# An attention and two-layer MoE kernel: scaled words in PSUM, joined maxima, numerator by head, and an order from a table

## The chip, the cores and the metric

The kernel runs on one core of a Trainium2 chip. The metric is the device time of one execution in microseconds (us), taken as the median of several runs.

## The reference

Random-feature attention gives the input of a gated MLP, whose output goes through eight experts with one expert per token. Cut to what matters (B 4, H 8, S 576, D 64, 128 features; 2304 tokens, model width 512, hidden widths 1536 and 1024; all float32):

```python
def phi(x):
    proj = np.einsum('bhsd,df->bhsf', x, w_phi)
    proj = proj - np.max(np.abs(proj), axis=-1, keepdims=True)
    return np.concatenate([np.exp(proj), np.exp(-proj)], axis=-1)
q_p, k_p = phi(q), phi(k)
kv = np.einsum('bhsf,bhsd->bhfd', k_p, v); z = np.sum(k_p, axis=2)
attn = np.einsum('bhsf,bhfd->bhsd', q_p, kv) / (np.einsum('bhsf,bhf->bhs', q_p, z)[..., None] + 1e-06)
x = attn.transpose(0, 2, 1, 3).reshape(B * S, H * D)
g = x @ moe_w_gate
x = (g / (1 + np.exp(-g)) * (x @ moe_w_val)) @ moe_w_out
# then, per token: e = argmax(x @ moe2_w_gate); gate * sigmoid(...) * relu(x @ w1[e]) @ w2[e]
```

## The kernel before

**Attention** goes by 16 units of two heads (u = 0 to 15; four units are one batch). A unit has: three *qk groups* (`qk_mm`, L286: projections of three 128-token tiles of q and of k into two PSUM banks); for each group the maximum of the absolute value and the subtraction on DVE (`amax` L294, `k_sub` L299, `q_sub` L309), where in the first part the q side of odd units takes its subtraction on ACT instead (`q_bias`, L314, three Identity instructions with a bias); two exponentials of the k side on ACT (`k_exp`); the *kv product* (`kv_mm`, L338 and L347) and its copy (`kv_copy`); three *transpose groups* of q (`tq_mm`, L365), each with two exponentials on ACT (`tq_exp`); the *numerator* (`num_mm`, L387 and L390), whose two banks hold six and four slices, since the tile shared by both heads is done for both; `normalise` (L403, L404, L407: an addition, a reciprocal and the products on DVE); the *output transposes* (`tx_mm`, L422), of which ACT keeps the rounded high part (`x_hi`) and DVE the rest (`x_lo`, L440).

**The gated MLP** goes by six blocks of 384 tokens (n) and twelve slices of the hidden width (f). Each slice has a *G product*, a *V product* (`gv_mm`, L540 to L542, 12 matmuls each) and an *o product* (`o_mm`, L578 to L580, 9 matmuls), each with a high and a low word of weights and of inputs. Between them lie `g_tanh` (ACT), `g_mul` (L552) and `v_mul` (L555) on DVE, `g_hi` (L558, ACT) and `g_lo` (L561), which makes the low word: on POOL in block 0, on DVE later. G and V have one bank each (3 and 4), the o products banks 0 to 2. Before a product, `split_hi` (L522, ACT) and `split_lo` (L526, POOL) cut the weights in two words; four buffers of each are in turn.

**Conversion.** The weights arrive as 64-bit words with three staging buffers (`conv_load`, SP). For each of 36 pieces ACT scales the high word into a buffer in SBUF (`conv_scale`, L491); the low word is rounded by POOL for the first eight pieces, by ACT for the others (`conv_round`, L498, L500); DVE joins sign and mantissa in two instructions (`conv_bits`, L504 and L505); POOL adds the two parts (`conv_add`, L509).

**The first part** (`first_part`) holds units 0 to 7, the qk groups of unit 8, all conversions and block 0 up to its last V product and the o product of slice 10. The G product of block 0 needs the outputs of units 0 to 3. Its order on PE, DVE, ACT and POOL is written by a planner (`Plan`): each step has a duration, a due time and what it reads and writes; at each turn the step that can start first is taken, among those that could start about then the one due first. Where PE would be idle for long before a certain time, a filler puts matmuls without use (L459). SP's loads are issued by the steps: `qk_mm` of the third group loads the next unit but one, `kv_mm` the values, `conv_load` the weights; SP takes them in one queue.

**After it** come blocks 1 to 5, into which units 8 to 15 are put step by step (`run_to`), then the routing and the expert slots.

Of the kernel before, what the change touches and what calls it, by code (L numbers as in the profile page):

```python
# [65 lines left out]


class Plan:
# [32 lines left out]
    def run(self, filler):
        ops = self.ops
        left = [len(o["deps"]) for o in ops]
        after = [[] for _ in ops]
        for i, o in enumerate(ops):
            for d in o["deps"]:
                after[d].append(i)
        end = [0.0] * len(ops)
        free = {}
        bank_free = [0.0] * 8  # L110
        ready = {i for i, n in enumerate(left) if n == 0}
        while ready:
            best = None
            for i in ready:
                o = ops[i]
                t = max([free.get(o["eng"], 0.0)] + [end[d] + self.LAT * (ops[d]["eng"] != o["eng"]) for d in o["deps"]])
                if o["banks"]:
                    b = sorted((bank_free[b], b) for b in o["pool"])[:o["banks"]]
                    if b[-1][0] == float("inf"):
                        continue  # L120
                    t = max(t, b[-1][0] + self.LAT)
                    o["take"] = [x[1] for x in b]
                cand = (t, o["due"], i)
                o["at"] = t
                if best is None or cand < best:
                    best = cand
            assert best is not None, "no op can be taken"
            same = [(ops[i]["due"], i) for i in ready if ops[i]["eng"] == ops[best[2]]["eng"]
                    and ops[i].get("at", 1e9) <= best[0] + 0.05 and (not ops[i]["banks"] or all(
# [997 lines left out]
```

## Time and profile before

| | us |
|---|---|
| median of 3 runs | 946.39 (945.83 to 946.68) |
| profiled execution | 945.33 |
| its span, first to last instruction | 943.6 |
| PE, DVE, ACT, POOL busy | 908.5, 640.8, 578.2, 404.6 |

The profile is that of one execution. A busy time says how long an engine had an instruction in work; matmuls are pipelined, and their modelled ends overlap, so the work of a group of matmuls is better read from its start to the start of the next group. Times in the trace are counted from the span's start.

### The profile page before, as it was taken

The numbers are of one execution on the slowest core, as the hardware profiler recorded it, in microseconds if no ns is written. First come the engines' busy times: TensorE is split into PE (matmuls) and PEld (weight loads), VectorE is DVE, ScalarE is ACT, GpSimd is POOL, SyncE is SP. The second block draws the span as 40 slices with busy tenths as digits, with TensorE's granted clock in tenths as the row PEclk, the third lists the DMA queues.
The fourth block names the chain that finished last, engine by engine and source line by source line (L and its number), as shares of the span: only waits on it lengthen the run. The fifth ranks groups of instructions, "written<-read, shape, count | busy, mean of one in ns | idle before, by whom it ended". The sixth has DMA issues, their size and how long they took to land.

```text
span 943.6 us, 18408 instructions
## 1 busy us (share of the span) xinstructions
PE 908.5 (96%) x7159; PEld 790.2 (84%) x7159; DVE 640.8 (68%) x1094; ACT 578.2 (61%) x1020; POOL 404.6 (43%) x324
## 2 busy tenths in 40 slices
PE   8998997999999999999999999989999999999995
PEld 5887886889999899988889999979877888887874
DVE  4899899645454744575564533565599988888984
ACT  4776876644545345454445344444588998888883
POOL 1459788735554344433435566566201111112210
PEclk9999999999999999999999999999999999999998
DMA  7555655120011101110000000054001137156240
GB/s 217 157 168 154 176 155 155 42 73 1 1 27 49 39 5 39 41 60 16 1 2 34 1 1 1 35 213 178 34 24 46 38 130 294 53 206 227 65 177 9
DMA packets 20939, 78.88 MB, mean 84 GB/s; under 512 B 5358, under 2 KB 5614, under 8 KB 19056
## 3 DMA queue, kind: packets, MB, share of 16 engines
q1 hardware_dynamic: 17280, 67.60, 22.2%
q0 software_dynamic: 3200, 9.48, 3.1%
q8 instruction: 58, 0.95, 0.4%
q10 hardware_dynamic: 368, 0.59, 0.2%
q14 instruction: 33, 0.27, 0.1%
HBM read 123.23 MB, written 10.00 MB: 141 GB/s over the span
## 4 chain that ended last, share of the span: by engine, by line
PE 76%; DVE 15%; issue 4%; DMA 3%; ACT 2%; POOL 0%; POOLq 0%; DVEq 0%; ACTq 0%
PE banks L915 10%; PE banks L540 10%; PE banks L542 9%; PE banks L541 9%; PE banks L578 5%; PE banks L579 5%; PE banks L580 5%; PE banks L286 3%; DVE arena L505 3%; PE banks L937 3%; PE banks L938 3%; PE banks L939 3%; DVE arena L504 2%; PE banks L347 2%; PE banks L390 2%
## 5 line engine op out<-in xcount | busy, mean ns | idle before, releaser
L526 POOL TENSOR_TENSOR arena_r<-arena,arena_r 128x512 fp32r<-128x512 f32 x216 | 285.8, 1325 | 247.2 <-ACT arena_r L522 234.4
L522 ACT ACTIVATE arena_r<-arena 128x512 fp32r<-128x512 f32 x216 | 135.9, 630 | 191.2 <-PE banks L541 109.7
L540 PE MATMUL banks<-arena_r 128*128 128x384 f32 x576 | 201.6, 350 | 1.7 <-DVE arena L552 1.0
L881 DVE TENSOR_TENSOR arena_r<-arena,arena_r 128x1024 fp32r<-128x1024 f32 x160 | 189.6, 1234 | 18.0 <-ACT arena_r L880 16.8
L542 PE MATMUL banks<-arena_r 128*128 128x384 f32 x576 | 193.9, 337 | 4.5 <-POOL arena_r L526 4.5
L541 PE MATMUL banks<-arena_r 128*128 128x384 f32 x576 | 193.4, 336 | 0.0
L880 ACT ACTIVATE arena_r<-arena 128x1024 fp32r<-128x1024 f32 x160 | 161.9, 1066 | 15.3 <-PE banks L915 10.9
L915 PE MATMUL banks<-arena_r 128*128 128x512 f32 x480 | 116.8, 396 | 0.0
L943 POOL DMA_INDIRECT out_dram<-arena x20 | 20.7, 1037 | 219.5 <-ACT arena L942 219.5
L540 PEld LDWEIGHTS banks<-arena_r 128*128 128x128 f32 x576 | 108.3, 188 | 7.8 <-issue 1.4
L542 PEld LDWEIGHTS banks<-arena_r 128*128 128x128 f32 x576 | 108.1, 188 | 5.8 <-POOL arena_r L526 5.8
L552 DVE SCALAR_TENSOR_TENSOR arena<-arena,banks 128x384 f32<-128x384 f32 x72 | 39.7, 552 | 107.6 <-ACT arena L549 107.5
L541 PEld LDWEIGHTS banks<-arena_r 128*128 128x128 f32 x576 | 108.5, 188 | 1.6
L915 PEld LDWEIGHTS banks<-arena_r 128*128 128x128 f32 x480 | 88.1, 188 | 20.2 <-ACT arena_r L907 2.1
L578 PE MATMUL banks<-arena_r 128*128 128x512 f32 x216 | 90.0, 417 | 0.0
L579 PE MATMUL banks<-arena_r 128*128 128x512 f32 x216 | 86.6, 401 | 0.0
L580 PE MATMUL banks<-arena_r 128*128 128x512 f32 x216 | 86.5, 402 | 0.0
L561 DVE TENSOR_TENSOR arena_r<-arena,arena_r 128x384 fp32r<-128x384 f32 x60 | 60.9, 1015 | 27.7 <-ACT arena_r L558 27.5
L294 DVE TENSOR_REDUCE arena<-banks 128x3 f32<-128x384 f32 x96 | 52.7, 554 | 23.6 <-PE banks L286 21.5
L555 DVE TENSOR_TENSOR arena<-arena,banks 128x384 f32<-128x384 f32 x72 | 39.8, 552 | 39.6 <-PE banks L542 38.8
L937 PE MATMUL banks<-arena_r 128*128 128x512 f32 x160 | 62.7, 392 | 1.0 <-ACT arena_r L880 0.7
L939 PE MATMUL banks<-arena_r 128*128 128x512 f32 x160 | 62.4, 390 | 0.0
(126 smaller groups left out, 1434.6 us busy)
## 6 DMA issues: line engine op xcount, KB each, us to landing
arena<-mw SPq DMA_DIRECT2D x40, 2048.0 KB
ov_conv<-w1cat SPq DMA_DIRECT2D x24, 512.0 KB
arena<-w1cat SPq DMA_DIRECT2D x12, 512.0 KB
arena<-v SPq DMA_DIRECT2D x16, 325.0 KB
x2d<-arena SPq DMA_DIRECT2D x18, 256.0 KB
arena<-qT SPq DMA_DIRECT2D x15, 288.0 KB
arena<-kT SPq DMA_DIRECT2D x15, 288.0 KB
ov_gather<-x2d,arena POOLq DMA_INDIRECT x20, 3.8
```

The lines of the kernel that those rows point to most:

```text
L522: ACT.activation(WH[i % 4], WR[f][w], AF.Copy)
L526: POOL.tensor_tensor(out=WL[i % 4], in0=WR[f][w], in1=WH[i % 4].bitcast(F32), op=ALU.subtract)
L540: PE.matmul(ps, wh[:, c], xh, start=(k == 0), stop=False)
L541: PE.matmul(ps, wh[:, c], xl, start=False, stop=False)
L542: PE.matmul(ps, wl[:, c], xh, start=False, stop=(k == 3))
L578: PE.matmul(ps, GH[f % 2][:, ts_], woh, start=(f == 0), stop=False)
L579: PE.matmul(ps, GH[f % 2][:, ts_], wol, start=False, stop=False)
L580: PE.matmul(ps, GL[f % 2][:, ts_], woh, start=False, stop=(f == NFT - 1))
L880: ACT.activation(h, src, AF.Copy)
L881: DVE.tensor_tensor(out=l, in0=src, in1=h.bitcast(F32), op=ALU.subtract)
L915: PE.matmul(PS[:, HB[h], :], lhs, w[:, h * 512:(h + 1) * 512], start=a, stop=b)
L937: PE.matmul(ps, HTH[:, k, :], wh[:, cs], start=(k == 0), stop=False)
```

## The change

- `conv_scale` writes the scaled word into a bank of PSUM, and `conv_bits` reads it there. The buffers CU go; CP becomes four buffers. The rounding runs on ACT or, where the table says so, on POOL.
- q and k of a qk group lie in two adjacent banks. One reduction takes the maxima of both, one subtraction serves both (`qk_sub`), into one tile KQ. `q_bias` goes. The sign of q's exponentials is exchanged accordingly.
- `num_mm` and `normalise` go by head, five slices each, with one bank each.
- `v_mul` writes its product back into the V bank; `g_hi` and `g_lo` read it there; `g_lo` is on DVE in all blocks.
- `Plan.run` no longer chooses: it takes the steps in the order of a list of 626 numbers, in which 1000 more than a step's number means its other engine (POOL for the rounding, DVE for the copy of kv). Durations and the delay between engines still serve to choose banks and fillers. A bank is chosen by when it comes free; outside the first part, by which was used longest ago.

With the table, DVE's order ahead of the first product of block 0 (now the V product) has 15 `qk_sub`, 9 `conv_bits`, 8 `normalise`, 8 `x_lo` and one copy of kv; PE's has 17 qk groups, 15 transpose groups, 5 kv products, the numerators and the output transposes of units 0 to 3. The second V product comes after three G products. The cut diff:

```diff
-NRP = 8
...
+PLAN_TABLE = [242, 247, 2, 1, 252, 0, 3, 4, 7, 5, 10, 13, 8, 6, 17, 33, 18, 11, 36, 9, 19, 20, 34, 39, 12, 21, 42, 22,
...
+    615, 606, 616, 617, 621, 613, 622, 614, 623, 618, 624, 619, 625, 620, 239, 240, 241]
...
+    def run(self, table, filler):
+        ops, lat = self.ops, self.LAT
+        end, on, free, bank_free = {}, {}, {}, [0] * 8
+        assert sorted(x % 1000 for x in table) == list(range(len(ops)))
+        for x in table:
+            i = x % 1000
             o = ops[i]
-            ready.discard(i)
-            filler(o["eng"], free.get(o["eng"], 0.0), o["at"])
+            eng, dur, fn = o["alt"] if x >= 1000 else (o["eng"], o["dur"], o["fn"])
+            assert all(d in end for d in o["deps"]), (i, o["deps"])
+            t = max([free.get(eng, 0)] + [end[d] + lat * (on[d] != eng) for d in o["deps"]])
             if o["banks"]:
-                o["holder"]["ps"] = [b for b in o["take"]]
-                for b in o["take"]:
-                    bank_free[b] = float("inf")
-                o["fn"](*o["take"])
-            elif o["holder"] is not None:
-                o["fn"](*o["holder"]["ps"])
-            else:
-                o["fn"]()
-            end[i] = o["at"] + o["dur"]
-            free[o["eng"]] = end[i]
+                if o["banks"] == 1:
+                    b = min(self.SINGLES, key=lambda b: max(t, bank_free[b] + lat))
+                else:
+                    b = min(self.PAIRS, key=lambda b: max(t, bank_free[b] + lat, bank_free[b + 1] + lat))
+                take = list(range(b, b + o["banks"]))
+                t = max([t] + [bank_free[b] + lat for b in take])
+            for b in o["claim"]:
...
+            fn(*(h["ps"][:1] if h is not None else ()))
+            on[i] = eng
+            end[i] = free[eng] = t + dur
...
-    CU = [buf(512) for _ in range(2)]
     CA = buf(512)
-    CP = [OV1[:, 2048:2560], buf(512)]
+    CP = [OV1[:, 2048:2560]] + [buf(512) for _ in range(3)]
...
+    def pair_no():
+        state["n"] += 1
+        b = min((b for b in state["banks"] if b + 1 in state["banks"]),
+                key=lambda x: (max(used[x], used[x + 1]), min(used[x], used[x + 1])))
+        used[b] = used[b + 1] = state["n"]
+        return b
...
-    def amax(b, m=MX):
-        ps3 = PS[:, b, :BT].rearrange("p (j f) -> p j f", f=P)
-        DVE.tensor_reduce(out=m, in_=ps3, axis=AX.X, op=ALU.max, apply_absolute_value=True)
-        return ps3, m.rearrange("p (j o) -> p j o", o=1).to_broadcast([P, 3, P])
-
-    def k_sub(u, c, b):
-        ps3, mb = amax(b)
-        DVE.tensor_tensor(out=KP[two(u)][:, 3 * c:3 * c + 3, 0:P], in0=ps3, in1=mb, op=ALU.subtract)
+    def qk_sub(u, c, b):
+
+        ps = PS[:, b:b + 2, :BT].rearrange("p w (j f) -> p w j f", f=P)
+        DVE.tensor_reduce(out=MX, in_=ps, axis=AX.X, op=ALU.max, apply_absolute_value=True)
+        t = KQ[two(u)][:, 3 * c:3 * c + 3, :].rearrange("p j (w f) -> p w j f", f=P)[:, 0:3:2]
+        m = MX.rearrange("p w (j o) -> p w j o", o=1).to_broadcast([P, 2, 3, P])
+        DVE.tensor_tensor(out=t, in0=ps, in1=m, op=ALU.subtract)
...
-    def q_sub(u, c, b):
-        ps3, mb = amax(b)
-        DVE.tensor_tensor(out=TQ[two(u)][:, 3 * c:3 * c + 3, :], in0=mb, in1=ps3, op=ALU.subtract)
-
-    def q_bias(u, c, b):
-        ps3 = PS[:, b, :BT].rearrange("p (j f) -> p j f", f=P)
-        for j in range(3):
-            ACT.activation(TQ[two(u)][:, 3 * c + j, :], ps3[:, j, :], AF.Identity, bias=MQ[c][:, j:j + 1], scale=-1.0)
...
+    def num_mm(u, h, b):
+
         kv = KV[u % 2]
-        for part, n in ((0, 6), (1, 4)):
-            ps = PS[:, banks[part], :n * 65].rearrange("p (s d) -> p s d", s=n)
-            for i in range(5 - part):
-                t = 5 * part + i
-                for a in range(2):
-                    for g in HALVES:
-                        q = qp(u)[:, a, t * P + g.start:t * P + g.stop]
-                        if t == 4:
-                            PE.matmul(ps[g, 4:6, :].rearrange("p s d -> p (s d)"), q, kv[:, a, :], start=(a == 0),
-                                      stop=(a == 1), skip_group_check=True)
-                        else:
-                            PE.matmul(ps[g, i, :], q, kv[:, a, part * 65:part * 65 + 65], start=(a == 0),
-                                      stop=(a == 1), skip_group_check=True)
+        ps = PS[:, b, :325].rearrange("p (s d) -> p s d", d=65)
+        for i in range(5):
+            for a in range(2):
+                for g in HALVES:
+                    t0 = h * S + i * P + (0 if i == 4 and h == 1 else g.start)
+                    PE.matmul(ps[g, i, :], qp(u)[:, a, t0:t0 + 64], kv[:, a, h * 65:h * 65 + 65], start=(a == 0),
+                              stop=(a == 1), skip_group_check=True)
...
+    def normalise(h, b):
+        ps = PS[:, b, :325].rearrange("p (s d) -> p s d", d=65)
+        rd = rot("rd", RD)[:, :5].rearrange("p (s o) -> p s o", o=1)
         DVE.tensor_scalar(out=rd, in0=ps[:, :, 64:65], scalar1=1e-6, scalar2=None, op0=ALU.add)
         DVE.reciprocal(out=rd, in_=rd)
-
-        def norm(dst, rows, s0, s1):
-            DVE.tensor_tensor(out=dst, in0=ps[rows, s0:s1, 0:64],
-                              in1=rd[rows, s0:s1].to_broadcast([rows.stop - rows.start, s1 - s0, 64]), op=ALU.mult)
-
-        lo, hi = slice(0, 64), slice(64, 128)
-        if part == 0:
-            norm(XT[:, 0:4, 0:64], slice(0, P), 0, 4)
-            norm(XT[lo, 4:5, 0:64], lo, 4, 5)
-            norm(XT[lo, 0:1, 64:128], hi, 5, 6)
-        else:
-            norm(XT[hi, 0:4, 64:128], lo, 0, 4)
-            norm(XT[lo, 1:5, 64:128], hi, 0, 4)
+        DVE.tensor_tensor(out=XT[:, :, h * 64:h * 64 + 64], in0=ps[:, :, 0:64], in1=rd.to_broadcast([P, 5, 64]), op=ALU.mult)
...
-    def conv_scale(i):
-        ACT.activation(CU[i % 2], ST[i % 3].rearrange("p (n two) -> p n two", two=2)[:, :, 1], AF.Copy,
+    def conv_scale(i, b):
+        ACT.activation(PS[:, b, :], ST[i % 3].rearrange("p (n two) -> p n two", two=2)[:, :, 1], AF.Copy,
                        scale=2.0 ** -112)
...
-        r = CP[i % 2].bitcast(I32)
-        if i < NRP:
+        r = CP[i % 4].bitcast(I32)
+        if eng is POOL:
...
-    def conv_bits(i):
-        ui, ai, wi = CU[i % 2].bitcast(I32), CA.bitcast(I32), WR[i // 3][i % 3].bitcast(I32)
+    def conv_bits(i, b):
+        ui, ai, wi = PS[:, b, :].bitcast(I32), CA.bitcast(I32), WR[i // 3][i % 3].bitcast(I32)
         DVE.tensor_scalar(out=ai, in0=ui, scalar1=-2 ** 31, scalar2=None, op0=ALU.bitwise_and)
         DVE.scalar_tensor_tensor(out=wi, in0=ui, scalar=3, in1=ai, op0=ALU.logical_shift_left, op1=ALU.bitwise_or)
...
-        DVE.tensor_tensor(out=GP, in0=GP, in1=PS[:, VB, :BT], op=ALU.mult)
+        DVE.tensor_tensor(out=PS[:, VB, :BT], in0=GP, in1=PS[:, VB, :BT], op=ALU.mult)
 
     def g_hi(f):
-        ACT.activation(GH[f % 2], GP, AF.Copy)
-
-    def g_lo(f, eng=DVE):
-        eng.tensor_tensor(out=GL[f % 2], in0=GP, in1=GH[f % 2].bitcast(F32), op=ALU.subtract)
+        ACT.activation(GH[f % 2], PS[:, VB, :BT], AF.Copy)
+
+    def g_lo(f):
+        DVE.tensor_tensor(out=GL[f % 2], in0=PS[:, VB, :BT], in1=GH[f % 2].bitcast(F32), op=ALU.subtract)
...
+                op("DVE", 190, lambda b, c=c: qk_sub(u, c, b), [("qk", u, c)] + tail, [("kp", z, c), ("tq", z, c)], holder=h, due=d0 + c)
+                op("ACT", 106, lambda c=c: k_exp(u, c), tail, [("kp", z, c)], due=d0 + c)
...
-            op("ACT", 0.69, due, lambda i=i: conv_scale(i), [("st", i % 3)], [("cu", i % 2)])
-            op("POOL" if i < NRP else "ACT", 1.65 if i < NRP else 0.69, due + 0.5, lambda i=i: conv_round(i), [("st", i % 3)], [("cp", i % 2)])
-            op("DVE", 1.75, due + 1, lambda i=i: conv_bits(i), [("cu", i % 2)], [("wr", i)])
-            op("POOL", 1.37, due + 3, lambda i=i: conv_add(i), [("cp", i % 2)], [("wr", i)])
+                op(("dma", i), 1400 + 300 * i, lambda: None, [], [("st", i % 3)])
+            h = op("ACT", 69, lambda b, i=i: conv_scale(i, b), [("st", i % 3)], [("cu", i)], 1, due=due)
+            op("ACT", 69, lambda i=i: conv_round(i, ACT), [("st", i % 3)], [("cp", i % 4)], due=due,
+               alt=("POOL", 162, lambda i=i: conv_round(i, POOL)))
+            op("DVE", 125, lambda b, i=i: conv_bits(i, b), [("cu", i)], [("wr", i)] + [("wrt",)] * (i >= 24), holder=h, due=due)
+            op("POOL", 137, lambda i=i: conv_add(i), [("cp", i % 4)], [("wr", i)], due=due)
...
-                op("DVE", 0.55, at + 1, v_mul, [("V",)], [("gp",)])
-                op("ACT", 0.53, at + 1.5, lambda f=f: g_hi(f), [("gp",)], [("gh", f % 2)])
-                op("POOL", 1.05, at + 2, lambda f=f: g_lo(f, POOL), [("gp",), ("gh", f % 2)], [("gl", f % 2)])
+                op("PE", 217, lambda f=f: gv_mm(0, f, 1), wts + xs, [("V",)], due=at)
+                op("DVE", 56, v_mul, [("gp",)], [("V",)], due=at)
+                op("ACT", 53, lambda f=f: g_hi(f), [("V",)], [("gh", f % 2)], due=at)
+                op("DVE", 60, lambda f=f: g_lo(f), [("V",), ("gh", f % 2)], [("gl", f % 2)], due=at)
...
-            ends = pl.run(filler)
+            pl.run(PLAN_TABLE, filler)
```

## Rows read from the trace of the kernel before

**Rows 1.** The page, part 1: busy us and share of the span by engine.

```profile
PE 908.5 (96%) x7159; PEld 790.2 (84%) x7159; DVE 640.8 (68%) x1094; ACT 578.2 (61%) x1020; POOL 404.6 (43%) x324
```

**Rows 2.** Windows: length, then busy us per engine, granted clock, DMA share, GB/s.

```profile
9.00:64.30 55.30, 50.64 (x914) 42.44 (x914) 47.82 (x108) 41.48 (x99) 22.22 (x16) 0.97 0.61 179
64.30:169.00 104.70, 92.84 (x816) 80.36 (x815) 98.19 (x142) 76.75 (x162) 88.52 (x66) 0.97 0.53 155
169.00:200.00 31.00, 31.00 (x308) 27.40 (x308) 18.69 (x38) 18.05 (x40) 18.47 (x15) 1.00 0.19 50
200.00:600.00 400.00, 399.32 (x3404) 362.72 (x3403) 204.13 (x441) 188.94 (x383) 189.84 (x149) 1.00 0.08 24
```

**Rows 3.** Timeline of PE: start us, length us, engine, line, count.

```profile
9.04 1.16 PE L286 MATMUL banks<-arena 64*128 64x128 f32 x16
...
64.31 0.42 PE L540 MATMUL banks<-arena_r 128*128 128x384 f32 x1
...
173.33 0.94 PE L286 MATMUL banks<-arena 64*128 64x128 f32 x12
174.20 0.55 PE L365 MATMUL banks<-arena 128*128 128x128 f32 x3
174.50 0.48 PE L578 MATMUL banks<-arena_r 128*128 128x512 f32 x1
...
180.65 0.45 PE L540 MATMUL banks<-arena_r 128*128 128x384 f32 x1
...
185.04 1.15 PE L390 MATMUL banks<-arena 128*64 128x65 f32 x32
...
187.50 0.50 PE L578 MATMUL banks<-arena_r 128*128 128x512 f32 x1
...
189.68 0.71 PE L422 MATMUL banks<-arena 128*128 128x128 f32 x5
```

**Rows 4.** Groups by line on PE, to 64.3 us, the last to 190.5 us.

```profile
L286 PE MATMUL banks<-arena 64*128 64x128 f32 x180 | 14.4, 296 | 1.7 <-ACT arena L314 1.3 <-ACT arena L370 0.3
L347 PE MATMUL banks<-arena 128*64 128x65 f32 x320 | 10.2, 221 | 0.0
L390 PE MATMUL banks<-arena 128*64 128x65 f32 x256 | 9.0, 223 | 0.0
...
L286 PE MATMUL banks<-arena 64*128 64x128 f32 x301 | 25.3, 295 | 4.2 <-DVE arena_r L440 2.5 <-ACT arena L314 1.3 <-ACT arena L370 0.3
```

**Rows 5.** Groups by line and shape, 0 to 200 us: busy us, mean ns.

```profile
L505 DVE SCALAR_TENSOR_TENSOR arena<-arena 128x512 int32<-128x512 int32 x36 | 44.5, 1236 | 1.2
L504 DVE TENSOR_SCALAR arena<-arena 128x512 int32<-128x512 int32 x36 | 33.0, 918 | 3.3 <-ACT arena L491 2.4
L294 DVE TENSOR_REDUCE arena<-banks 128x3 f32<-128x384 f32 x54 | 29.4, 552 | 16.0 <-PE banks L286 14.8
...
L314 ACT ACTIVATE arena<-banks,arena 128x128 f32<-128x128 f32 x36 | 10.4, 360 | 0.5 <-DVE arena L294 0.5
...
L440 DVE TENSOR_TENSOR arena_r<-banks,arena_r 128x192 fp32r<-128x192 f32 x16 | 5.2, 349 | 1.9 <-ACT arena_r L436 1.8
...
L440 DVE TENSOR_TENSOR arena_r<-banks,arena_r 128x384 fp32r<-128x384 f32 x4 | 2.2, 554 | 1.3 <-ACT arena_r L436 1.3
...
L404 DVE RECIPROCAL arena<-arena 128x6 f32<-128x6 f32 x8 | 1.5, 192 | 0.3
```

**Rows 6.** Timeline of DVE, one pair of conv_bits.

```profile
62.71 0.43 DVE L504 TENSOR_SCALAR arena<-arena 128x512 int32<-128x512 int32 x1
63.17 1.66 DVE L505 SCALAR_TENSOR_TENSOR arena<-arena 128x512 int32<-128x512 int32 x1
```

**Rows 7.** Timeline of POOL at the same time.

```profile
63.01 1.27 POOL L526 TENSOR_TENSOR arena_r<-arena,arena_r 128x512 fp32r<-128x512 f32 x1 [1.05 <-ACT arena_r L522]
```

**Rows 8.** Groups by line on DVE, 200 to 600 us.

```profile
L715 DVE COPY arena<-banks 128x512 f32<-128x512 f32 x13 | 9.0, 691 | 10.1 <-PE banks L714 10.1
```

**Rows 9.** Timelines of DVE and PE in a later block: g_lo, the next V product.

```profile
307.63 1.14 DVE L561 TENSOR_TENSOR arena_r<-arena,arena_r 128x384 fp32r<-128x384 f32 x1 [0.59 <-ACT arena_r L558]
...
315.08 0.44 PE L540 MATMUL banks<-arena_r 128*128 128x384 f32 x1
```

More of the change, by code (lines that the diff above doesn't have):

```diff
@@ L97, in op @@
             holder["users"] += 1
-        self.ops.append(dict(eng=eng, dur=dur, due=due, fn=fn, deps=deps, banks=banks, pool=pool, holder=holder))
+        self.ops.append(dict(eng=eng, dur=dur, fn=fn, deps=deps, banks=banks, holder=holder, claim=claim, alt=alt, due=due))
         return holder
[L101 to L129, printed above, removed]
-                        bank_free[b] < float("inf") for b in ops[i].get("take", ())))]
-            i = min(same)[1]
@@ new lines, in run @@
+                take = list(range(b, b + o["banks"]))
+                t = max([t] + [bank_free[b] + lat for b in take])
+            for b in o["claim"]:
+                t = max(t, bank_free[b] + lat)
+            assert t < self.NEVER, "no bank"
+            filler(eng, free.get(eng, 0), t)
+            for b in o["claim"]:
+                bank_free[b] = self.NEVER
+            h = o["holder"]
+            if o["banks"]:
+                h["ps"] = take
+                for b in take:
+                    bank_free[b] = self.NEVER
@@ L152, in run @@
                         bank_free[b] = h["end"]
-            for j in after[i]:
-                left[j] -= 1
-                if left[j] == 0:
-                    ready.add(j)
-        assert not any(left)
-        self.end = end
-        return free
+            if PLAN_LOG is not None:
+                PLAN_LOG.append((i, eng, t, dur))
 @with_exitstack
@@ L335, in kv_mm @@
                 for g in HALVES:
-                    lhs = KP[two(u)][:, t, a * P + g.start:a * P + g.stop]
+                    lhs = KQ[two(u)][:, t, a * P + g.start:a * P + g.stop]
                     if i == 0:
@@ L613, in unit @@
[L613 to L616 removed]
+            h = op("PE", 242, lambda b: kv_mm(u, b), [("kp", z, c) for c in range(3)] + [("v", u)] + tail,
+                   [("kvm", u)], 1, due=d0 + 8)
@@ L617, in unit @@
+            for p_ in range(2):
+                h = op("PE", 122, lambda b, p_=p_: num_mm(u, p_, b),
+                       [("qp", z, c) for c in ((0, 1), (1, 2))[p_]] + [("kv", u % 2)] + tail, [("num", u, p_)], 1,
+                       due=d0 + 14)
+                op("DVE", 85, lambda b, p_=p_: normalise(p_, b), [("num", u, p_)], [("xt", p_), ("xt2", p_)],
+                   holder=h, due=d0 + 14)
             for part in range(2):
```

159 lines of the change are left out of this document (72 added, 87 removed), and 25 rows, old and new, of the table PLAN_TABLE.

## The prediction

> **What bounds the kernel now.** I read the page first: PE is busy in 96% of the span [rows 1], so only time in which PE works on nothing needed can be won. The windows say where that is [rows 2]. From 200 to 600 us PE is busy 399.32 of 400 us: nothing to win. From 9 to 64.3 us and from 64.3 to 169 us it isn't, and there DVE is busy 47.82 of 55.3 and 98.19 of 104.7 us (94%), the highest share of any engine behind PE. From 169 us DVE falls to 18.69 of 31 and PE is at 31.00 of 31. So the first part is held by DVE until about 169 us, and then by PE.
>
> PE's busy time counts filler matmuls and overlapped ends, so I count from start to start in a dense stretch [rows 3]: a qk group (12 records) 174.20 - 173.33 = 0.87 us, a transpose group 174.50 - 174.20 = 0.30, two G or V products 185.04 - 180.65 = 4.39, so 2.19 each, a numerator 187.50 - 185.04 = 2.46 (a kv product has as many matmuls of the same widths and is taken at 2.46 too), an o product 189.68 - 187.50 = 2.18, a unit's output transposes 0.71.
>
> The first G product starts at 64.31, the last o product of the first part ends at 189.68 [rows 3]. By 64.3 us 180 qk records (15 groups) and the kv records of five units (320) and numerator records of four (256) are done, by 190.5 us 301 (25 groups) [rows 4]. Between the two marks PE had 24 x 2.19 + 11 x 2.18 + 10 x 0.87 + 3 x 2.46 (kv) + 4 x 2.46 (num) + 9 x 0.30 + 3 x 0.71 = 107.3 us of work in 125.4 us: it lost 18.1 us. Two qk groups and one unit's transposes of the first part are still owed then (2.4 us), so its work ends, in effect, at 192.1.
>
> **The change part by part.** DVE prices come from one view [rows 5]. An instruction with one PSUM operand takes 349 ns at 128x192 and 554 at 128x384, so 205 ns for 192 elements more: by that line 128x320 is 0.49 us, 128x512 0.69, 128x768 0.96.
>
> *Scaled words in PSUM.* The two instructions of conv_bits take 918 and 1236 ns on average, 77.5 us in all, and they vary: 0.43 and then 1.66 us in one pair [rows 6]. During the long one POOL ran a subtraction on SBUF words, 63.01 to 64.28 [rows 7]. With the scaled word in PSUM neither instruction reads two SBUF words any more. I take 0.691 (a 128x512 copy out of PSUM [rows 8]) for the first and 0.69 for the second: 1.38 against 2.15, 36 x 0.77 = 27.9 us less on DVE. Bounds: 1.12 (0.43 + 0.69) and 2.15; the copy is the nearest row. Here a rule speaks against the change: the Trainium skill, VectorE: DVE Perf Modes, section "Why PSUM operands drop a tier", says that an fp32 operand in PSUM holds such an instruction to the single rate. By that rule it is 0.69 and not the 0.43 of the SBUF form, and the copy's 0.691 agrees; with 0.43 the first G product would come 9 x 0.26 = 2.3 us sooner than below. ACT's write into PSUM has no row; ACT is busy for 76.75 of 104.7 us [rows 2], and 0.1 us more or less on 36 of them is 3.6 us that it has.
>
> *One maximum for k and q.* A group was two reductions (552) and two subtractions of the same width, 2.2 us on DVE in even units; in odd units DVE did 1.65 and ACT three Identity instructions of 360 ns. It becomes 2 x 0.96 = 1.93 in all units. ACT loses 36 x 0.36 = 13.0 us [rows 5]. Over 27 groups DVE is about even.
>
> *Numerator by head.* 40 records of 65 columns per head instead of 32 and 8 wider ones: PE about even. A normalise is two short instructions, each at most the reciprocal's 192 ns, and one 128x320 product of 0.49: 0.87 us, twice a unit.
>
> *g_lo from POOL to DVE in the first block, product in PSUM.* 12 x 0.55 = 6.6 us more for DVE, and POOL loses 12 instructions. In later blocks the DVE instruction with its two SBUF sources (1.14 us at 307.63 [rows 9]) goes towards 0.55; hidden, since DVE is busy in half of that stretch [rows 2]. The V bank now stays taken until g_lo has read it; who waits is a rival below. A DVE write into PSUM has no row; 0.55 is the nearest, up to 0.69.
>
> *The table.* It sets the order on PE, DVE, ACT and POOL. I summed the instructions that it puts ahead of two marks. Before the first product of the block (now a V product): DVE has 15 groups x 1.93, 9 conv_bits x 1.38, 8 normalise x 0.87, 8 x_lo (4 x 0.554, 4 x 0.349) and one kv copy of 0.42: 52.4 us. PE has only 44.2 there (17 qk, 15 transpose groups, 5 kv, 4 num, 4 output transposes). DVE's first input is there some 0.9 us after PE's first qk at 9.04, so at 10.0. With DVE at the 94% that it reaches today, 52.4 takes 55.7: the first product starts at 65.7, no sooner than now, with more of the weights converted. Bounds: 62.4 (no idle) and 70.9 (the 86% of today's stretch up to 64.3). I take 94% because conversions now stand between the attention steps to fill DVE's waits.
>
> After that mark PE has 24 x 2.19 + 11 x 2.18 + 10 x 0.87 + 3 x 2.46 + 4 x 2.46 + 9 x 0.30 + 4 x 0.71 = 108.0 us, DVE 12 x 1.93 + 27 x 1.38 + 8 x 0.87 + 12 x 0.349 + 36 x 0.554 + 3 x 0.42 = 92.9, or 86% of PE's time. What PE loses lies between 0 (169 to 200 us [rows 2]) and today's 18.1. Up to the second V product both have about 21.5 us to do, so at 94% DVE is 1.4 behind; then PE has 86 us against 71 on DVE, and I allow 3 more: 4.5 lost.
>
> SP's loads move with the PE steps that issue them and with the conversions that free their buffers; SP holds them in one queue in the table's order. Bytes are the same in some 7% less time, and the queues carried 179 GB/s at a share of 0.61 in the first stretch [rows 2], so I price this at nothing; a late load would show as an ACT wait at conv_scale.
>
> **Sum.** 65.7 + 108.0 + 4.5 = 178.2 instead of 192.1: 13.9 us less. Behind it PE has no gap to swallow that before 600 us, and the later waits hang on PE's own progress, so all of it reaches the end. The profiled execution took 945.33 us (span 943.6), so 931.4; the median of the runs, 946.39, lies 1.1 above it: 932.5.
>
> **The rivals.** *The waits come back.* A fixed order is right for one set of durations; where ACT, POOL or a load is late, PE waits in line. For it: ACT gets as tight as DVE, since its exponentials and conversions are also packed ahead of the first product. Against: with no pair stretched by POOL, durations vary less. If half of the 13.6 us of waits that I take away returns, 939; if all, 946.
>
> *The pair gets no cheaper in PSUM* (2.15 stays). Then DVE has 6.9 more before the mark (59.3, at 94% a start at 73.1) and 20.8 more behind it, 113.7 us, over PE's 108.0; at 94% 121.0: end at 194.1, 948. Against it: the forms that read PSUM lie on one line (349, 552, 554 ns [rows 5]) beside a POOL that is busy for 88.52 of 104.7 us [rows 2].
>
> *No idle at all:* 62.4 + 108.0 = 170.4, 21.7 us less: 925.
>
> *Slower: the V bank.* The next V product must now wait for g_hi and g_lo. In a later block g_lo is done at 308.77 and the next V product begins at 315.08 [rows 9], 6.3 us of room. At the closest, one G and one o product (4.37 us) lie between two V products, against a chain of three instructions of some 0.55 us and the steps from engine to engine. If DVE's queue, where a 1.93 us group may stand in front, carries the chain beyond 4.37, each of 60 V products waits; the gain is gone at 13.9 / 60 = 0.23 us each, and at 0.5 us it is 932.5 + 30 = 962.5. Against it: those 6.3 us, and that g_lo gets shorter.
>
> **How the numbers follow.** Forecast 0.68 (its own range 926 to 938), waits back 0.14, no idle 0.10, V bank 0.05, pair no cheaper 0.03. Two in a thousand is about what a measurement of this kernel can tell from no change. Faster by more than that: 0.68 + 0.10 + 0.11 of the returned waits = 0.89; same 0.04; slower 0.07. The range 921 to 942 takes in the forecast, the case with no idle and the milder half of the returned waits.
>
> **What would show it.** Right: conv_bits near 1.38 a pair with little spread; first product of the block at 62 to 70 us; last o product of the first part at 174 to 181; DVE below 90% after the first third of that stretch; 200 to 600 us unchanged. Wrong: a pair above 1.8; PE waits on ACT or POOL of over 8 us between the marks; V products waiting for g_lo in the later blocks; the clock granted below 1.0 in more slices than now.

## The result, and the profile after

| | us, median | runs | ratio to before | 95% interval |
|---|---|---|---|---|
| before | 946.11 | 945.59 to 946.68 | | |
| after | 933.99 | 929.81 to 936.30 | 0.9867 | 0.9828 to 0.9905 |

The forecast was 932.5 us in a range of 921 to 942. The profiled execution of the changed kernel took 929.81 us (span 927.9), the fastest of the four. Its windows, as in [rows 2]: length, then busy us of each engine, granted clock, DMA share, GB/s.

```profile
9.00:64.30 55.30, 46.58 (x857) 38.83 (x857) 44.97 (x70) 38.23 (x83) 13.01 (x10) 0.97 0.60 173
64.30:169.00 104.70, 103.33 (x1138) 93.38 (x1137) 86.98 (x156) 78.11 (x159) 85.58 (x67) 1.00 0.54 169
169.00:200.00 31.00, 31.00 (x258) 28.06 (x257) 10.70 (x19) 14.78 (x29) 16.30 (x13) 1.00 0.18 56
200.00:600.00 400.00, 399.92 (x3424) 363.28 (x3423) 173.61 (x398) 186.31 (x385) 191.59 (x151) 1.00 0.07 21
```

The second line is the gain: PE 103.33 of 104.7 us where it was 92.84, DVE 86.98 where it was 98.19. The first line is worse than before: PE 46.58 instead of 50.64 and DVE 44.97 instead of 47.82 of 55.3 us. The timeline of PE gives the marks that answer to [rows 3].

```profile
10.01 0.38 PE L302 MATMUL banks<-arena 64*128 64x128 f32 x2
...
70.04 0.45 PE L531 MATMUL banks<-arena_r 128*128 128x384 f32 x1
...
177.75 0.94 PE L302 MATMUL banks<-arena 64*128 64x128 f32 x12
178.62 0.45 PE L531 MATMUL banks<-arena_r 128*128 128x384 f32 x1
...
184.74 0.39 PE L571 MATMUL banks<-arena_r 128*128 128x512 f32 x1
```

First qk group at 10.01, first product of block 0 at 70.04, the last qk group of the first part ends, by the start of what follows, at 178.62. Below I compare kernels by one later mark that all of them share, the end of block 0's last o product (start plus length of its last matmul): some 185 us here, by the last row above, and 199.40 in the kernel before.

```profile
199.01 0.39 PE L580 MATMUL banks<-arena_r 128*128 128x512 f32 x1
```

Prices by line and shape, 0 to 200 us (busy us, mean ns, then idle time before), beside [rows 5]:

```profile
L314 DVE TENSOR_TENSOR arena<-banks,arena 128x768 f32<-128x768 f32 x27 | 25.8, 957 | 1.0
L311 DVE TENSOR_REDUCE arena<-banks 128x6 f32<-128x768 f32 x27 | 25.7, 953 | 16.8 <-PE banks L302 16.2
L496 DVE SCALAR_TENSOR_TENSOR arena<-banks,arena 128x512 int32<-128x512 int32 x36 | 24.9, 691 | 1.2
L495 DVE TENSOR_SCALAR arena<-banks 128x512 int32<-128x512 int32 x36 | 24.7, 686 | 7.0 <-ACT banks L482 6.2
L482 ACT ACTIVATE banks<-ov_conv 128x512 f32<-128x512 f32 x24 | 15.3, 640 | 11.8 <-DMA ov_conv<-w1cat 6.9 <-DVE arena L314 2.0 <-PE banks L394 1.5
L408 DVE TENSOR_TENSOR arena<-banks,arena 128x320 f32<-128x320 f32 x16 | 7.9, 491 | 0.6
L546 DVE TENSOR_TENSOR banks<-arena,banks 128x384 f32<-128x384 f32 x14 | 7.8, 558 | 4.1 <-PE banks L533 4.1
L552 DVE TENSOR_TENSOR arena_r<-banks,arena_r 128x384 fp32r<-128x384 f32 x14 | 7.7, 552 | 4.5 <-ACT arena_r L549 4.5
```

PE's waits from the first product to 178.6 us are down to two (us in total, times, longest), 1.1 us in all:

```profile
PE banks L413 <- DVE arena L408: 0.6, 1, 0.6
PE banks L302 <- ACT arena L379: 0.5, 1, 0.5
```

What stands out ahead of the first product is a late load. Timelines of ACT and of SP's queue (start, length; an idle time and its releaser in brackets):

```profile
37.39 0.62 ACT L482 ACTIVATE banks<-ov_conv 128x512 f32<-128x512 f32 x1 [4.95 <-DMA ov_conv<-w1cat]
```

```profile
26.79 0.33 SPq L479 DMA_DIRECT2D arena<-w1cat  x1
28.02 0.33 SPq L292 DMA_DIRECT2D arena<-v  x1
28.88 0.47 SPq L289 DMA_DIRECT2D arena<-qT  x1
29.45 0.55 SPq L286 DMA_DIRECT2D arena<-kT  x1
30.08 1.02 SPq L479 DMA_DIRECT2D ov_conv<-w1cat  x2
```

Weight tile 4 is issued only at 30.08, behind V of unit 3 and q and k of unit 4, which PE first uses at 54.70 and 51.23 us. ACT stood for 4.95 us, DVE's conv_bits behind it for 2.3 and a transpose on PE for 2.7.

### The profile page after: what moved, and what is told of

Read it like the earlier page. It is cut to its first block, busy times and chain, and to the rows that moved or that the text cites. A ratio compares the mean times of both kernels' runs of the same rounds, so it can differ in the third digit from the quotient of the medians.

```text
span 927.9 us, 18397 instructions
## 1 busy us (share of the span) xinstructions
PE 899.0 (97%) x7271; PEld 786.4 (85%) x7273; DVE 572.9 (62%) x978; ACT 563.6 (61%) x981; POOL 384.3 (41%) x310
## 4 chain that ended last, share of the span: by engine, by line
PE 85%; DVE 5%; DMA 4%; issue 3%; ACT 2%; POOL 0%; POOLq 0%; DVEq 0%; ACTq 0%; SPq 0%
PE banks L531 11%; PE banks L533 10%; PE banks L532 10%; PE banks L903 10%; PE banks L569 5%; PE banks L571 5%; PE banks L570 5%; PE banks L394 4%; PE banks L302 4%; PE banks L352 3%; PE banks L925 3%; PE banks L926 3%; PE banks L927 3%; DMA ov_gather<-x2d,arena 2%; PE banks L914 2%
## 5 line engine op out<-in xcount | busy, mean ns | idle before, releaser
L517 POOL TENSOR_TENSOR arena_r<-arena,arena_r 128x512 fp32r<-128x512 f32 x216 | 281.7, 1307 | 251.3 <-ACT arena_r L513 243.3
L869 DVE TENSOR_TENSOR arena_r<-arena,arena_r 128x1024 fp32r<-128x1024 f32 x160 | 189.1, 1230 | 18.1 <-ACT arena_r L868 16.9
L903 PE MATMUL banks<-arena_r 128*128 128x512 f32 x480 | 117.0, 396 | 0.0
L531 PEld LDWEIGHTS banks<-arena_r 128*128 128x128 f32 x576 | 108.6, 189 | 4.5
L569 PE MATMUL banks<-arena_r 128*128 128x512 f32 x216 | 87.8, 406 | 0.0
L571 PE MATMUL banks<-arena_r 128*128 128x512 f32 x216 | 85.3, 396 | 0.0
L570 PE MATMUL banks<-arena_r 128*128 128x512 f32 x216 | 85.3, 395 | 0.0
L546 DVE TENSOR_TENSOR banks<-arena,banks 128x384 f32<-128x384 f32 x72 | 40.3, 560 | 39.8 <-PE banks L533 39.6
L925 PE MATMUL banks<-arena_r 128*128 128x512 f32 x160 | 62.7, 392 | 1.0 <-ACT arena_r L868 0.7
L311 DVE TENSOR_REDUCE arena<-banks 128x6 f32<-128x768 f32 x48 | 45.7, 953 | 27.4 <-PE banks L302 26.8
L927 PE MATMUL banks<-arena_r 128*128 128x512 f32 x160 | 62.4, 390 | 0.0
L926 PE MATMUL banks<-arena_r 128*128 128x512 f32 x160 | 62.4, 390 | 0.0
```

The lines of the kernel that those rows point to most:

```text
L517: POOL.tensor_tensor(out=WL[i % 4], in0=WR[f][w], in1=WH[i % 4].bitcast(F32), op=ALU.subtract)
L531: PE.matmul(ps, wh[:, c], xh, start=(k == 0), stop=False)
L569: PE.matmul(ps, GH[f % 2][:, ts_], woh, start=(f == 0), stop=False)
L570: PE.matmul(ps, GH[f % 2][:, ts_], wol, start=False, stop=False)
L571: PE.matmul(ps, GL[f % 2][:, ts_], woh, start=False, stop=(f == NFT - 1))
L869: DVE.tensor_tensor(out=l, in0=src, in1=h.bitcast(F32), op=ALU.subtract)
```

## The experiments

Theory 1: words in PSUM relieve DVE and carry the gain; the table only packs. Theory 2: the table's order carries it. In the table below, "first" is the start of block 0's first product and "end" the end of its last o product in the profiled execution. The first mark carries some scatter: the first qk group starts when the fillers that open the kernel end, and the same 28 of them end at 10.01 us in the changed kernel, 9.04 in the kernel before and 8.88 in e_sbuf_words. Where it matters, the time from the first qk group to the first product is given too.

| run | us | ratio, 95% interval | first | end |
|---|---|---|---|---|
| before | 946.1 to 946.7 | 1 | 64.31 | 199.40 |
| after | 933.99 | 0.9867 (0.9828 to 0.9905) | 70.04 | 185.14 |
| e_greedy | 924.62 | 0.9771 (0.9749 to 0.9794) | 58.42 | 177.63 |
| e_greedy_sbuf | 940.58 | 0.9933 (0.9899 to 0.9968) | 60.08 | 194.85 |
| e_sbuf_words | 940.88 | 0.9945 (0.9922 to 0.9967) | 69.77 | 192.81 |
| b_words | 931.99 | 0.9846 (0.9829 to 0.9862) | 71.04 | 185.77 |
| e_greedy_two_max | 928.85 | 0.9815 (0.9794 to 0.9835) | 61.12 | 180.78 |
| e_greedy_gp | 923.88 | 0.9762 (0.9737 to 0.9787) | 58.60 | 178.11 |
| e_load_order | 928.26 | 0.9814 (0.9789 to 0.9840) | 68.40 | 183.90 |
| e_lo_fill | 924.97 | 0.9768 (0.9752 to 0.9784) | 66.30 | 181.32 |
| e_early_x0 | 932.86 | 0.9874 (0.9851 to 0.9897) | 71.29 | 186.98 |
| e_table_queue | 931.67 | 0.9853 (0.9818 to 0.9887) | 65.74 | 181.84 |
| e_queue_only | 922.20 | 0.9747 (0.9730 to 0.9764) | 56.25 | 176.27 |
| e_one_queue | 915.93 | 0.9676 (0.9656 to 0.9697) | 54.11 | 172.23 |

**The other steps without the table: e_greedy.**

```diff
-        for x in table:
-            i = x % 1000
+        while ready:
...
+            i = min((ops[i]["due"], i) for i in ready
+                    if ops[i]["eng"] == ops[best[2]]["eng"] and ops[i]["at"] <= best[0] + 5)[1]
```

> All steps of the changed kernel (words in PSUM, one maximum, numerator by heads, g_lo on VectorE), but the first part is again put in order by the rule of the kernel before: earliest start, then due time, with its bank sets for each unit; rounding of tiles 0 to 7 on GpSimd, of the others on ScalarE, as before. Theory 1 (the relief of VectorE carries the gain; the table only packs): the pair of conv_bits stays at 1.38 us, the first product of block 0 starts at 60 to 68 us, and the stretch behind it loses 3 to 8 us of TensorE instead of 0.6; 932 to 940 us. Theory 2 (the order carries the gain): waits return as in the kernel before, some 18 us of TensorE lost behind the first product; 943 to 949 us.

924.62 us: below the ranges of both theories, and 9.4 faster than with the table. So theory 2 falls, and with it the premise that the table helps. More than the order goes back: the old rule has its own bank sets, POOL rounds pieces 0 to 7 and ACT makes every kv copy, while the table gives POOL seven pieces, one of them among the first eight, and DVE four copies. What each of these is worth was not tried. Windows of e_greedy:

```profile
9.00:64.30 55.30, 50.29 (x890) 43.19 (x893) 51.71 (x86) 44.01 (x95) 30.53 (x23) 1.00 0.73 216
64.30:169.00 104.70, 104.70 (x1138) 93.84 (x1138) 78.11 (x139) 78.23 (x155) 76.67 (x61) 1.00 0.47 144
```

DVE works 51.71 of 55.3 us in the first stretch, against 44.97 with the table.

**The words alone, in three settings: e_sbuf_words (table), e_greedy_sbuf (old rule), b_words (kernel before).** The first two put the words into the WR tile where they end:

```diff
-        ACT.activation(PS[:, b, :], ST[i % 3]
+        ACT.activation(WR[i // 3][i % 3], ST[i % 3]
...
-        ui, ai, wi = PS[:, b, :].bitcast(I32), CA
+        ui, ai, wi = WR[i // 3][i % 3].bitcast(I32), CA
```

> The table's order and every other step of the changed kernel, but the scaled high words lie in SBUF, in the tile of WR that they end in, so both instructions of conv_bits read SBUF. Theory 1 (the words in PSUM make the pair cheap, and VectorE is what the stretch waits for): the pair goes back from 1.38 to 1.9 to 2.2 us, VectorE takes 19 to 28 us more in the first part, some 9 of them ahead of the first product of block 0; that product starts at 76 to 80 instead of 70 us, and the time is 938 to 948 us. Theory 2 (order carries the gain): VectorE has the room, the first product moves by under 2 us; 930 to 937 us.

> The steps of the changed kernel in the order of the old rule (the run e_greedy, 924.6 us), but the scaled high words lie in SBUF (in their tile of WR); every engine has the same list in the same order as in e_greedy. Theory 1 (words in PSUM carry the gain, since VectorE has next to no idle time ahead of the first product there): 36 pairs cost 0.54 to 0.77 us more each; 8 to 10 pairs lie ahead of the first product of block 0, so it starts 5 to 8 us later than 58.4 us, and behind it TensorE waits a little: 931 to 937 us. Rival (the gain comes from the one maximum, the numerator by heads and g_lo): under 3 us, 924 to 928 us.

b_words does the reverse in the kernel before, `CU[i % 2]` becoming `PS[:, b, :]` with a bank from the planner.

> The kernel before with one part of the change alone: the scaled high words go to a bank of PSUM (bank 5 to 7, for the first nine tiles also 0 to 2), two in flight at most as before. Theory 1 (the words carry most of the gain, 16 of some 22 us as the runs e_greedy and e_greedy_sbuf differ): the pair falls from 2.15 to 1.38 us, the 18 us that TensorE loses behind the first product shrink to 4 to 8: 930 to 936 us. Rival (without the numerator by heads, which needs one bank at a time, the words take banks that q, k and the numerator wait for): the pair is cheap but TensorE waits for banks, 938 to 946 us.

The words are worth 6.9 us in the table's order, 16.0 in the old rule's, and 14.3 alone in the kernel before, no less than the whole change brought (12.1). The direction fits theory 1 and the size in two of the runs; 940.58 is more than the 931 to 937 of the third. The place does not fit: without the words the first product starts 0.3 us sooner and 1.7 us later, counted from the first qk group 0.9 and 0.7 later, not 5 to 10 later. In b_words, with the words in PSUM, it even starts 6.7 us later than in the kernel before, with ten pairs ahead of it instead of six, and the gain lies wholly behind it. The windows of e_greedy_sbuf show where the loss is:

```profile
9.00:64.30 55.30, 49.67 (x888) 42.46 (x890) 50.55 (x82) 42.63 (x93) 29.30 (x21) 1.00 0.73 208
64.30:169.00 104.70, 93.67 (x910) 82.94 (x909) 91.28 (x127) 69.64 (x139) 79.38 (x58) 0.97 0.45 141
```

PE falls from 104.70 to 93.67 in the second stretch, and all that it waits for behind the first product is DVE:

```profile
PE banks L398 <- DVE arena L393: 5.3, 2, 3.0
PE banks L287 <- DVE arena_r L416: 3.1, 2, 1.8
PE banks L516 <- DVE arena_r L537: 1.7, 1, 1.7
PE banks L516 <- DVE arena L528: 0.9, 1, 0.9
```

That is 11.0 us, against none in e_greedy; in e_sbuf_words it is 6.9 us, again all on DVE. The clock adds to it: granted at 0.97 in that stretch instead of 1.00, an estimated 3 us ((1 - 0.97) x 104.7). b_words shows the same the other way round: PE's waits behind the first product are 0.5 us there and were 11.7 in the kernel before. Why the loss lies there is in DVE's timeline of e_greedy_sbuf, an early pair and a later one, with POOL's at the later time:

```profile
26.41 0.42 DVE L480 TENSOR_SCALAR arena<-arena 128x512 int32<-128x512 int32 x1
26.86 0.69 DVE L481 SCALAR_TENSOR_TENSOR arena<-arena 128x512 int32<-128x512 int32 x1
...
65.42 1.32 DVE L480 TENSOR_SCALAR arena<-arena 128x512 int32<-128x512 int32 x1
66.78 1.66 DVE L481 SCALAR_TENSOR_TENSOR arena<-arena 128x512 int32<-128x512 int32 x1
```

```profile
65.18 1.28 POOL L485 TENSOR_TENSOR arena<-arena 128x512 int32<-128x512 int32 x1 [0.70 <-ACT arena_r L498]
66.42 3.16 POOL L502 TENSOR_TENSOR arena_r<-arena,arena_r 128x512 fp32r<-128x512 f32 x2
```

The early pair takes 1.11 us, less than the 1.38 from PSUM; the later one, beside POOL, 2.98. Over all 36 pairs, by overlap of the two timelines: the second instruction takes 0.69 us in the 13 cases without POOL beside it and 1.36 on average in the other 23, the first 0.42 (6 cases) and 0.90 (30). The eight pairs ahead of the first product sum to 11.0 us, 1.38 each, what PSUM costs; the 28 behind it to 58.8, 2.10 each. From PSUM there is no such difference: minimum, median and maximum in e_greedy (first two lines) and in e_greedy_sbuf:

```profile
L480 DVE TENSOR_SCALAR arena<-banks x36: 678/682/693, 20.5 to 140.4; 128x512 int32<-128x512 int32 x36
L481 DVE SCALAR_TENSOR_TENSOR arena<-banks,arena x36: 690/691/692, 21.2 to 141.1; 128x512 int32<-128x512 int32 x36
```

```profile
L480 DVE TENSOR_SCALAR arena<-arena x36: 415/716/1551, 21.4 to 157.4; 128x512 int32<-128x512 int32 x36
L481 DVE SCALAR_TENSOR_TENSOR arena<-arena x36: 691/694/1719, 21.9 to 159.0; 128x512 int32<-128x512 int32 x36
```

The Trainium skill, SBUF — State Buffer, section "Who interferes with whom", says that a DVE instruction with two SBUF inputs contends with a GpSimd (POOL) instruction that reads SBUF. The trace agrees for the second instruction, 1.36 against 0.69 us. The first has one SBUF input and slows as well, which that sentence does not cover.

**The other two parts, under the old rule.** e_greedy_two_max:

```diff
-        DVE.tensor_reduce(out=MX, in_=ps, axis=AX.X, op=ALU.max, apply_absolute_value=True)
+        for w in range(2):
+            ps = PS[:, b + w, :BT].rearrange("p (j f) -> p j f", f=P)
+            DVE.tensor_reduce(out=MX[:, w, :], in_=ps, axis=AX.X, op=ALU.max, apply_absolute_value=True)
```

> As e_greedy, but each group of q and k has a reduction and a subtraction for each of its two banks, four instructions of 0.55 us instead of two of 0.95. Theory 1: 2.2 instead of 1.91 us a group, some 13 groups ahead of the first product, so it starts 3.5 to 4 us later, and the time is 927 to 930 us. Rival (a group's end is what TensorE waits for, and k alone is ready sooner with two subtractions): no change, 922 to 926 us.

4.2 us more, in the range of theory 1; the first product starts 2.7 later, less than its 3.5 to 4. The two intervals just touch. e_greedy_gp:

```diff
-        DVE.tensor_tensor(out=PS[:, VB, :BT], in0=GP, in1=PS[:, VB, :BT], op=ALU.mult)
+        DVE.tensor_tensor(out=GP, in0=GP, in1=PS[:, VB, :BT], op=ALU.mult)
...
+                op("POOL", 105, lambda f=f: g_lo(f, POOL), [("gp",), ("gh", f % 2)], [("gl", f % 2)], due=at)
```

> As e_greedy, but the gated product of the first part goes back to its SBUF tile: the product with V writes SBUF, the low part g_lo is taken on GpSimd from SBUF, and the bank of V is free after the product. Theory 1 (the stretch behind the first product is bound by TensorE, 104.7 of 104.7 us busy): VectorE gets back 12 x 0.55 us that nobody waits for, GpSimd takes 12 x 1.1 us more; 923 to 928 us, no change that counts. Rival (GpSimd's weight parts come late behind the g_lo): TensorE waits for GpSimd 3 us or more, 928 to 934 us.

No difference that can be measured: DVE has room behind the first product (72.95 us of 104.7 here, 78.11 in e_greedy). The numerator by head was not tried alone. e_greedy lies 7.4 us under b_words, the words alone; the joined maxima account for 4.2 of that, and the rest is not placed.

**Why the table is slower: e_load_order, e_lo_fill, e_early_x0, e_table_queue.** e_load_order moves two entries of the table's loads ahead of the kv product and the qk group that issue the others.

> The table with one thing moved: the loads of weight tiles 4 and 3 are issued ahead of the loads of V for unit 3 and of q and k for unit 4; the order of every compute engine is as in the table. Theory 1 (ScalarE's wait of 4.95 us at 37 us is a transfer queued behind transfers nobody needs yet): the wait goes, and TensorE's 2.7 us behind it; the first product of block 0 starts at 65 to 67.5 instead of 70.0 us, time 926 to 932 us. Rival (the wait hides work that the stretch needs anyway: VectorE or the next chain is late next): ScalarE's wait goes but the first product stays within 1.5 us of 70 us, time as the changed kernel, 930 to 936 us.

ACT's wait goes (1.0 us for a load remains), and the median falls by 5.7 us, in intervals that overlap slightly. But in the profiled executions the first product starts only 1.6 us sooner (1.1 from the first qk group), short of the 65 to 67.5 expected, and block 0 ends 1.2 us sooner; the rest of the 5.7 us is not placed. A part of the gain is lost to the clock: for 6.8 us from 19.2 us on it was granted at 0.50, the level of 1.2 GHz. The window of that spell in e_load_order, and the same one in the next run, e_lo_fill:

```profile
19.20:26.00 6.80, 6.19 (x49) 5.12 (x51) 4.14 (x6) 3.82 (x9) 0.00 (x0) 0.50 0.27 79
```

```profile
19.20:26.00 6.80, 6.27 (x106) 5.02 (x106) 5.46 (x8) 4.93 (x11) 0.00 (x0) 1.00 0.30 78
```

```diff
-            if eng == "PE" and t1 < 6000 and t1 - t0 > 90:
-                warmup((t1 - t0 - 30) // 40)
+            if eng == "PE" and t1 < 6000 and t1 - t0 > 25:
+                warmup(max(1, (t1 - t0 - 30) // 40) + (t0 > 0))
```

> As e_load_order (table, two weight loads moved ahead), with filler products of TensorE in every planned gap of 0.25 us or more of the first 60 us, instead of 0.9 us, some 20 more fillers of 0.2 to 0.4 us. In e_load_order the granted clock was 0.5 for 6.8 us from 19.2 us on, which cost 3.4 us. Theory (the clock fell because TensorE stood idle in that stretch): no half-speed spell between 10 and 70 us, 924 to 927 us. Rival (the fillers only push the chain behind them, the clock falls as before or the gaps it fills are not the real ones): 927 to 932 us.

With the gaps filled, by 25 more fillers up to 72 us, the clock stays at 1.00, the first product starts 2.1 us sooner and the time falls another 3.3 us: the theory on the clock holds. From 12.3 to 19.2 us PE had been busy for 4.34 of 6.9 us in e_load_order and for 6.05 in e_lo_fill.

e_early_x0 only lowers the planner's arrival times of the first inputs.

> The planner is told that the first inputs are there at 1.5, 5, 7 and 10.5 us of its clock instead of 7, 10.5, 12.5 and 16, so that it puts 14 fewer filler products ahead of the first product of q and k, which then starts at about 5.5 instead of 10.0 us; the table is unchanged. If the start of the chain sets the first stretch: the first product of block 0 starts 3 to 5 us earlier (65 to 67 us), time 926 to 931 us. Rival (transfers of weights and later inputs set it, or the clock falls for want of fillers): under 1.5 us gained, or a half-speed stretch shows in the first 20 us; 930 to 938 us.

The rival was right. PE starts at 6.17 instead of 10.01, and then waits in line for inputs, longest for those of unit 2; behind that wait the clock fell too, to 0.51 from 18.8 to 25.6 us:

```profile
PE banks L302 <- DMA arena<-qT: 5.1, 2, 3.9
PE banks L302 <- DMA arena<-kT: 1.5, 2, 1.0
```

e_table_queue keeps the table for the four compute engines and issues all loads from a list of its own (`LOADS`, by position in the table).

> The table's order of every compute engine, but loads issued in the order in which the table first uses them, each as soon as its buffer is free and the queue has room at about 215 GB/s; tiles 0 to 2 and V of unit 1 come behind the inputs of unit 2, and 14 fewer fillers stand ahead of the first product, as in e_one_queue (915.9 us). Theory 1 (what the table loses to the old rule it loses through transfers that its search took for independent, and through the clock): 915 to 922 us, as e_one_queue. Rival (the order of the compute engines itself is worse on the chip): no better than e_load_order's 928.3 us by more than 4, so 924 to 930 us.

Theory 1 falls, and 931.67 lies above the rival's range of 924 to 930 as well, no better than after, though the end of block 0 comes 3.3 us sooner; the later stages ran with more half-speed spells in that execution, of which this window is the longest:

```profile
604.50:611.30 6.80, 5.54 (x28) 4.67 (x28) 2.63 (x9) 1.12 (x2) 3.39 (x4) 0.50 1.02 379
```

So loads are not the whole of it: with the loads in order, the table ends block 0 5.6 and 9.6 us later than the next two kernels. Which of its steps does that was not tried.

**A version that beats both: e_queue_only and e_one_queue.** The old rule, with every load an operation of one queue in the planner, as long as its bytes at about 215 GB/s (the first window of e_greedy shows 216):

```diff
-                op("SP", 10, lambda i=i: conv_load(i), [], [("st", i % 3)], due=due - 8)
-                op(("dma", i), 400, lambda: None, [], [("st", i % 3)])
+            op("Q", 240, lambda i=i: conv_load(i), [], [("st", i % 3)], due=due - 8)
+            op(("dma", i), 180, lambda: None, [], [("st", i % 3)])
```

e_one_queue sets prices and due times anew besides (for instance units 0 to 3 due every 8.4 instead of 11 us, conv_bits 1.38 instead of 1.25). It also takes the rounding of pieces 0 to 7 from POOL to ACT, which its expectation does not say:

```diff
-            op(*(("POOL", 165, lambda i=i: conv_round(i, POOL)) if i < 8 else ("ACT", 69, lambda i=i: conv_round(i, ACT))),
+            op(*(("POOL", 165, lambda i=i: conv_round(i, POOL)) if i < 0 else ("ACT", 69, lambda i=i: conv_round(i, ACT))),
```

> As e_greedy, but all loads of the first part are operations of one queue in the planner, each as long as its bytes at about 215 GB/s, and are issued in its order; weight tiles 1 and 2 and V of unit 1 are loaded behind the inputs of unit 2; the first inputs are expected at 1.5 us of the planner's clock instead of 7 (so 14 fewer fillers ahead of the first product of q and k); due times and prices are set anew for that. Theory 1 (what is left to gain lies ahead of the first product, in the start of the chain and in late transfers): first product of q and k at 5.5 to 6.5 us, first product of block 0 at 52 to 56 us instead of 58.4, time 917 to 922 us. Rival (transfers bound the start, or the clock falls where the fillers are gone): TensorE waits 3 us or more for transfers, or more half-speed spells; 922 to 928 us.

> As e_one_queue, but with the due times and prices of e_greedy; only the loads are planned on one queue and the first inputs expected earlier. If queue and early start carry the 8.7 us between e_greedy and e_one_queue: 916 to 920 us. If the new due times do: 921 to 925 us.

Queue and earlier start give 2.4 us, in overlapping intervals, so e_queue_only falls in its second range; due times, prices and the rounding on ACT together another 6.3, so these carry more of it, and which of the three is not separated. e_one_queue, at 915.93 us just below the range expected, is 3.2% under the kernel before. Its windows:

```profile
9.00:64.30 55.30, 52.30 (x990) 46.28 (x988) 50.31 (x85) 46.12 (x101) 16.59 (x13) 1.00 0.72 203
64.30:169.00 104.70, 104.55 (x1044) 93.95 (x1044) 82.36 (x145) 80.75 (x164) 78.35 (x63) 1.00 0.51 153
```

PE is busy for 52.30 us in the first stretch, 5.72 more than with the table.

## Why the prediction was right, and where it was not

**Right in the sum.** 178.62 for 178.2 at the end of the first part, 929.81 for 931.4 in the profiled execution, 933.99 for 932.5 in the median, and 200 to 600 us unchanged. The four executions spread by 6.5 us, so a hit within 2 us is in part luck.

**Prices.** conv_bits 686 + 691 = 1.38 us as taken, every one between 0.68 and 0.69. A qk group 1.91 for 1.93, a normalise 0.157 + 0.191 + 0.491 = 0.84 for 0.87, g_lo 0.55 for 0.55, the write into PSUM by DVE 0.56, by ACT 0.64. The rule of the Trainium skill that was weighed there (VectorE: DVE Perf Modes, section "Why PSUM operands drop a tier") holds too: the first instruction takes 0.69 from PSUM and 0.42 from SBUF without POOL beside it. One reading was off, without weight in the sum: q_bias is busy for 10.4 us on ACT in [rows 5], not 36 x 0.36 = 13.0.

**Where the saving lies.** The prediction spread 0.77 us evenly over 36 pairs, 6.9 of it ahead of the first product. The average of [rows 5] mixed two stages. The groups of the kernel before, cut at its first product, show it:

```profile
L505 DVE SCALAR_TENSOR_TENSOR arena<-arena 128x512 int32<-128x512 int32 x6 | 5.5, 911 | 0.2
L504 DVE TENSOR_SCALAR arena<-arena 128x512 int32<-128x512 int32 x6 | 3.1, 517 | 0.1
```

Six pairs at 0.911 + 0.517 = 1.43 us, next to nothing over PSUM; so the 30 behind, out of 77.5 us in all, cost (77.5 - 8.6) / 30 = 2.30 each, and nearly all of the saving, 30 x 0.92 = 27.6 us, lies there, where DVE was at 94%. The rival "pair no cheaper" put 2.15 on every pair and reached 948 us. In e_sbuf_words, its nearest run, the pair took 1.92 on average, 1.54 in the ten ahead of the first product and 2.06 behind it, and the time was 940.9.

**First product: 65.7 said, 70.04 measured**, inside the bounds of 62.4 to 70.9. The step that failed is DVE's 94% there. Its work was about as counted, 52.4 us in the sum of its groups, but over the stretch that the prediction means DVE was busy for 50.42 of 60.04 us, 84%:

```profile
10.00:70.04 60.04, 51.03 (x954) 43.27 (x956) 50.42 (x82) 42.77 (x92) 14.29 (x11) 0.97 0.58 169
```

The 4.3 us have several sources. The first qk group started 0.97 us later than the 9.04 that was taken over from the kernel before. From it to the first product it took 60.03 us, where 56.7 were forecast. With the two loads moved this falls to 58.90 (e_load_order), with the gaps filled besides to 57.13 (e_lo_fill). So the term "loads priced at nothing" and the clock, to which the sum gave no term, account for 2.9 of these 3.4 us; moving the loads alone gave 1.1, since the clock then fell for 6.8 us instead of 3.4. The remaining 0.5 us and the later start stay open. A table that fixes the order on PE fixes SP's too. The sign that the prediction named, an ACT wait at conv_scale, is the row at 37.39.

**Loss behind it: 4.5 said, 0.6 measured** (178.62 - 70.04 is 108.6, against 108.0 of work). No V product waits, and PE's waits are 1.1 us, so the 108.0 is counted a little high. DVE was at 83% from 64.3 to 169 us instead of 94%; in e_sbuf_words it is at 92% there (96.81 of 104.7 us), and PE's waits for it are back. The two errors, 4.3 and 3.9 us, cancel: the total is better than its parts, by luck.

The 18.1 us that the kernel before lost were not waits alone, which the prediction did not say. PE's waits between its two marks sum to 11.7 us, the three largest being

```profile
PE banks L542 <- POOL arena_r L526: 4.5, 3, 3.0
PE banks L286 <- DVE arena_r L440: 2.5, 2, 2.1
PE banks L422 <- DVE arena L407: 2.3, 1, 2.3
```

and the clock was granted at 0.97 from 64.3 to 169 us [rows 2], an estimated 3 us ((1 - 0.97) x 104.7). In the changed kernel it is 1.00, so a part of the gain behind the first product is the clock that no longer falls there.

**What was not asked.** The prediction took the table's order and never asked what the same steps cost under the old rule; e_greedy puts 9.4 us on that question. The rival "waits come back" had the mechanism (a load late, PE in line), but as a loss behind the first product.

## What to carry to other kernels

A mean price can hide two stages: split it by what the other engines do at the time before multiplying it. Where DVE and POOL work on SBUF side by side, moving an operand of such a pair to PSUM paid here (1.38 instead of 2.1 to 2.3 us); without POOL beside it the pair took 1.11 from SBUF, and it would not have. A fixed order is no better than its model: here the transfers were one gap in it, and not the only one. After every change of prices, run the plain rule with the new prices beside it. Compare marks within a kernel from a common start, and read the granted clock beside every wait.

## What the runs showed of the hardware

The four runs of the changed kernel differ by 6.5 us and order themselves by the granted clock, 929.81 us at 0.993, 932.62 at 0.990, 935.36 at 0.988, 936.30 at 0.986: 0.007 of 930 us is 6.5 us. One spell in the profiled execution (window as above), behind PE's wait at 36.8 to 39.5 us:

```profile
40.80:44.20 3.40, 2.96 (x40) 2.27 (x40) 2.67 (x6) 2.90 (x8) 1.28 (x1) 0.50 0.03 7
```

So an idle gap ahead of dense work can cost twice, once as the gap and once as a lower level behind it, and 25 more fillers took the second cost away in e_lo_fill.
